# Retention and feed-forward on one core: the opening of the kernel reordered

## Chip, core and metric

The kernel runs on one NeuronCore of a Trainium2 chip. The metric is the device time of one execution in microseconds. The kernel before was timed in three runs; the profile is of a further execution. Engines are named as in the profile: PE is TensorE (PEld its weight loads), DVE VectorE, ACT ScalarE, POOL GpSimd, SP SyncE, which here only issues DMAs.

## What is computed

Attention without softmax and with a decay (retention), then a feed-forward layer of two products with `h - tanh(h)` between them. Batch 8, 8 heads, 576 positions, head size 64, so 4608 tokens of 512 numbers; the hidden size is 2048. All data is float32.

```python
scores = scale * np.matmul(q, k.transpose(0, 1, 3, 2))       # scale = 1/8
gamma = 1.0 - 2.0 ** (-5.0 - np.arange(H))
Dmat = np.where(rel >= 0, gamma[:, None, None] ** rel, 0.0)  # rel = query position - key position
x = np.matmul(scores * Dmat, v)      # then laid out as [tokens, heads * 64]
h = x @ w_in
out = (h - np.tanh(h)) @ w_out
```

## The kernel before

**Blocks and items.** The 576 positions are nine chunks of 64. A block is one chunk for all eight batches, 512 tokens. An item is one chunk of one batch with its eight heads. Items of chunk 0 need no state; later ones use a running state (the sum of k times v over earlier chunks), which is held in SBUF as `state`. Two items of one chunk make a pair; pairs 4 to 7 belong to block 1, pairs 8 to 11 to block 2, and so on. An *entry* (`entry`, line 253) does one pair on TensorE: the scores of the next pair, the outputs of this pair, its share of the state and, where asked for, first states of chunk 0 (`first_states`). Behind it DVE and ACT make the masked scores `pm` and the split output `xh`, `xl`.

**Two words for a number.** TensorE's matmuls here read fp32r. Each operand of the feed-forward products is split into a high word and a low remainder, and three products of these are summed. A hidden step `mm1(n, f)` (line 285) multiplies hidden tile f of 16 for block n: 12 matmuls, then a copy of the result by ACT (line 296) and, for block 0 and most of block 1, a DMA of it to DRAM (the *spill*, line 297), from where it is fetched later. The second product is `mm2` (line 330).

**Weights.** A weight tile is 512 KB, loaded by `load_w` (line 68). ACT makes a mask from it (`guard`, lines 74 and 75); DVE builds the high word in three instructions (lines 83, 88 and 90), ACT copies it (line 93) and DVE makes the low word (line 100). This is one *unit*, given out in three steps by `step()`; the low word of a unit is issued behind line 83 of the next one (`finish`). At its second step a unit also issues the next tile's guard, if that tile's load has been issued by then (line 86); otherwise the next guard comes with the next unit's first step. `stream` lists the 32 tiles, first those of `w_in`.

**Order.** Instructions keep, on every engine, the order in which they are written (`in_order`), and so do the DMAs in an issuing queue. The opening handles chunk 0 item by item (lines 405 to 417), with tile 0 converted between items 4 to 7, then tile 1. Then a list `seq` of 32 hidden steps runs (line 441): block 0's alone for the first `lead` = 10 steps, then block 0's and block 1's in turn. In step k, ahead of `mm1`: loads up to tile k + 5 (from k = 4), scalings of v and k by ACT (`scale_v`, `scale_k`), the first step of unit k + 2; behind it: the other two steps, loads by the table `loads` in steps 0 to 3, and an entry in steps 5, 6, 8 and 9 (the table `early`). The scores of pair 4 and the first states of the first two batches come in step 3. Scaling q of pairs 4 to 8 is POOL's work.

**Tiles that share a place.** Early data lies where the second weights will be later: items of chunk 0 in wo15 down to wo8, decay in wo7, the table for q in wo6, the k rows of chunk 0 in wo4 and wo5, pairs 6 and 7 in wo0 to wo3.

## Time and profile before

| | |
|---|---|
| timed runs | 904.4, 905.46, 903.27 us; median 904.4 us |
| profiled execution | 902.73 us, its span 901.0 us |
| granted TensorE clock, mean | 0.995 |
| PE busy | 880.7 us, 98% of the span |
| DVE / ACT / POOL busy | 367.7 / 288.8 / 74.3 us |
| DMA | 82.06 MB, mean 91 GB/s |

The span runs from the first to the last instruction; 1.7 us of the execution lie around it. Rows of the timeline give the start, the duration, the engine and line, the operation with its output and inputs, and in brackets how long the engine sat idle before it and what ended that. A clock of 1.00 is full speed.

### The profile page before, as it was taken

The page shows a single profiled execution, that of the slowest core. Times are in us where ns is not written, and L with a number is a line of the kernel's source. Part 1 is how long each engine was busy: PE and PEld are TensorE (multiplying, and loading weights), DVE is VectorE, ACT ScalarE, POOL GpSimd, SP SyncE. Part 2 cuts the span into 40 slices and gives each one's busy share as a digit, 9 for nine tenths or more (in the row PEclk, how much of TensorE's full clock was granted, in tenths as well). Part 3 has the DMA queues.
Part 4 walks back from the last instruction along what each step waited for, and adds up shares of the span by engine and source line. Part 5 has one row for each costly group of instructions (what it writes and reads, how often), then busy time and mean ns, then how long its engine had stood idle before and what let it go on. Part 6 is the DMA issues. An engine that isn't in the chain of part 4 may idle for free.

```text
span 901.0 us, 17598 instructions
## 1 busy us (share of the span) xinstructions
PE 880.7 (98%) x7834; PEld 725.5 (81%) x7834; DVE 367.7 (41%) x547; ACT 288.8 (32%) x514; POOL 74.3 (8%) x66
## 2 busy tenths in 40 slices
PE   7879999999999999999999999999999999999997
PEld 5668888878888888888888888888888888888886
DVE  5778968665332333223323332333333322223222
ACT  3668865444222222122222222222222222222222
POOL 0220001120010011111111111110001111000000
PEclk9989999999999999999999999999999999999999
DMA  8975864462311121111311131113110211002001
GB/s 318 330 259 197 292 216 130 153 206 83 95 48 53 40 55 48 53 48 51 91 54 48 47 95 54 48 47 95 48 48 21 77 49 48 1 1 48 1 1 47
DMA packets 30844, 82.06 MB, mean 91 GB/s; under 512 B 3760, under 2 KB 4912, under 8 KB 30768
## 3 DMA queue, kind: packets, MB, share of 16 engines
q1 hardware_dynamic: 30448, 80.41, 27.7%
q8 instruction: 61, 1.00, 0.5%
q10 hardware_dynamic: 320, 0.52, 0.2%
q14 instruction: 15, 0.12, 0.0%
HBM read 63.62 MB, written 17.30 MB: 90 GB/s over the span
## 4 chain that ended last, share of the span: by engine, by line
PE 95%; DMA 1%; DVE 1%; issue 1%; ACT 1%; SPq 0%; DVEq 0%
PE o L343 44%; PE h L291 43%; PE s L218 3%; PE own L218 2%; PE new L218 2%; DMA rwi<-in_w_in_dram 1%; DMA a<-in_first_dram 0%; PE new_first L218 0%; DVE mi L88 0%; PE s_first L218 0%; ACT wi L93 0%; DVE mi L90 0%; DVE ob L358 0%; PE wps L372 0%; ACT mi L74 0%
## 5 line engine op out<-in xcount | busy, mean ns | idle before, releaser
L291 PE MATMUL h<-xh,wi 128*128 128x512 f32 x1152 | 306.3, 391 | 3.7 <-ACT wi L93 2.8
L343 PE MATMUL o<-wo,gh 128*128 128x512 f32 x1152 | 293.4, 393 | 0.4 <-DVE ob L358 0.4
L291 PEld LDWEIGHTS h<-xh,wi 128*128 128x128 f32 x1152 | 216.0, 188 | 50.3 <-ACT wi L93 4.2
L343 PEld LDWEIGHTS o<-wo,gh 128*128 128x128 f32 x1152 | 213.8, 188 | 46.8 <-DVE ob L358 1.5
L305 DVE TENSOR_TENSOR g<-h,g 128x512 f32<-128x512 f32 x114 | 78.8, 691 | 370.2 <-ACT g L304 370.2
L304 ACT ACTIVATE g<-h 128x512 f32<-128x512 f32 x114 | 68.2, 598 | 423.8 <-PE h L291 422.9
L343 PE MATMUL o<-wo,gl 128*128 128x512 f32 x576 | 158.3, 389 | 0.0
L291 PE MATMUL h<-xl,wi 128*128 128x512 f32 x576 | 154.7, 391 | 0.0
L291 PEld LDWEIGHTS h<-xl,wi 128*128 128x128 f32 x576 | 108.7, 189 | 22.8
L343 PEld LDWEIGHTS o<-wo,gl 128*128 128x128 f32 x576 | 108.1, 188 | 22.5
L307 DVE TENSOR_TENSOR gl<-g,gh 128x512 fp32r<-128x512 f32 x114 | 82.4, 723 | 78.2 <-ACT gh L306 71.4
L306 ACT CAST gh<-g 128x512 fp32r<-128x512 f32 x114 | 70.7, 620 | 87.9 <-DVE g L305 87.9
L154 POOL TENSOR_TENSOR a<-a,qtab 128x512 f32<-128x512 f32 x28 | 36.9, 1317 | 637.7 <-DMA a<-in_qkv_dram 571.7
L218 PE MATMUL own<-a,state 64*64 64x64 f32 x960 | 59.2, 221 | 0.0
L218 PE MATMUL own<-pm,a 64*64 64x64 f32 x960 | 57.7, 218 | 0.0
L218 PEld LDWEIGHTS own<-a,state 64*64 64x64 f32 x960 | 47.8, 134 | 0.4 <-issue 0.4
L218 PEld LDWEIGHTS own<-pm,a 64*64 64x64 f32 x960 | 48.0, 135 | 0.0
L218 PEld LDWEIGHTS s<-a 64*64 64x64 f32 x960 | 30.5, 134 | 10.9 <-issue 10.9
L218 PE MATMUL s<-a 64*64 64x64 f32 x960 | 34.7, 221 | 0.3 <-issue 0.3
L327 DVE TENSOR_TENSOR gl<-s,gh 128x512 fp32r<-128x512 f32 x30 | 21.9, 730 | 29.8 <-PE o L343 27.3
L155 POOL TENSOR_TENSOR a<-a,vtab 128x512 f32<-128x512 f32 x28 | 31.4, 1122 | 0.0
L326 ACT CAST gh<-s 128x512 fp32r<-128x512 f32 x30 | 18.7, 622 | 38.6 <-PE o L343 27.9
(57 smaller groups left out, 476.9 us busy)
## 6 DMA issues: line engine op xcount, KB each, us to landing
a<-in_qkv_dram SPq DMA_DIRECT2D x30, 1024.0 KB, 5.3
out_dram<-ob SPq DMA_DIRECT2D x68, 128.0 KB, 2.4
rwi<-in_w_in_dram SPq DMA_DIRECT2D x16, 512.0 KB, 8.2
rwo<-in_w_out_dram SPq DMA_DIRECT2D x16, 512.0 KB, 4.7
spill_dram<-g SPq DMA_DIRECT2D x30, 256.0 KB, 3.1
s<-spill_dram SPq DMA_DIRECT2D x30, 256.0 KB, 2.8
a<-in_first_dram SPq DMA_DIRECT2D x8, 384.0 KB, 6.0
a_early<-in_qkv_dram SPq DMA_DIRECT2D x4, 512.0 KB, 7.2
```

The source lines that it names most:

```text
L154: nc.gpsimd.tensor_tensor(a[:, :, 0], a[:, :, 0], qtabs[c].unsqueeze(1).broadcast_to([P, 2, 4, C]), op=ALU.mult)
L155: nc.gpsimd.tensor_tensor(a[:, :, 2], a[:, :, 2], vtab[:, c].unsqueeze(1).unsqueeze(3).broadcast_to([P, 2, 4, D]), op=ALU.mult)
L218: nc.tensor.matmul(out_, w, x, start=start, stop=stop)
L291: nc.tensor.matmul(hp, win[f][:, a, cc, :], x[:, cc, :], start=(k == 0), stop=(k == 3 * NCC - 1))
L304: nc.scalar.activation(g, h, AF.Tanh)
L305: nc.vector.tensor_tensor(g, h, g, op=ALU.subtract)
L306: nc.scalar.copy(gh, g)
L307: nc.vector.tensor_tensor(gl, g, gh.bitcast(F32), op=ALU.subtract)
L326: nc.scalar.copy(gh, g)
L327: nc.vector.tensor_tensor(gl, g, gh.bitcast(F32), op=ALU.subtract)
L343: nc.tensor.matmul(o[t], g[:, t * P : (t + 1) * P], wout[f][:, a, :], start=(f == first and k == 0), stop=(f == final and k == 2),)
```

## The change

**Opening.** Item 1 and the decay table are loaded from ACT's queue; the activation that loads ACT's table comes after these issues and after the warm-up matmuls. Tile 0 is loaded behind item 3 instead of behind item 4; its guard comes at item 2, its three steps at items 3, 4 and 5. The k rows of the first four batches are loaded ahead of tile 2, and tile 3 is the last load of the opening.

**Order.** `lead` is 13, so block 1's hidden steps begin at step 13 of the list. Entries come in steps 4, 7, 10 and 12; the scores of pair 4 and first states in step 2. Tile 4 is issued in step 0, tile 5 in step 1 and none in step 2; in steps 3 to 8 one tile is issued in each, tile k + 3, behind the spill of the step; from step 9 on, ahead of `mm1`, loads go up to tile k + 4. Pair 5 is loaded in step 0, pair 6 in step 3, pair 7 in step 6, pair 8 in step 8 and pair 9 in step 13. The second k rows come in step 2.

**Engines.** q of pairs 4 to 8 is scaled by DVE, one instruction a pair, in steps 1, 3, 6, 9 and 11. Pairs 6 and 7 are loaded as two tiles that hold both items, one with q and k, one with v and the k rows, so that one instruction spans both items. The k rows are scaled four batches at a time, in steps 1 and 5. The copies of first states into `state` are ACT's.

```diff
+class Parts:
+    def __init__(self, parts):
+        self.parts = parts
+    def __getitem__(self, at):
+        return self.parts[at[1] // 2][at[0], at[1] % 2, at[2], at[3]]
...
-    def prep(p):
+    def prep(p, q=True):
...
+        if q:
+            table = qtabs[c].unsqueeze(1).broadcast_to([P, 2, 4, C])
+            nc.gpsimd.tensor_tensor(a[:, :, 0], a[:, :, 0], table, op=ALU.mult)
...
+        src = qkv_d[c - 1, 2 * pr : 2 * pr + 2].rearrange("u p t i s -> p u t i s")
+        parts = []
+        for t in range(2):
+            parts.append(const.tile([P, 2, 2, 4, C], F32, tag=f"wo{2 * (pr - 2) + t}", name=f"a_early{p}_{t}"))
+            nc.sync.dma_start(parts[t], src[:, :, 2 * t : 2 * t + 2])
         for u in range(2):
-            j = 2 * p + u
-            loaded[j] = const.tile([P, 4, 4, C], F32, tag=f"wo{2 * (pr - 2) + u}", name=f"a_early{j}")
-            nc.sync.dma_start(loaded[j], qkv_d[c - 1, 2 * pr + u])
+            loaded[2 * p + u] = Parts([part[:, u] for part in parts])
+        loaded["qv", p] = parts[0][:, :, 0], parts[1][:, :, 0]
 
     def scale_q(p):
-        if ("pair", p) in loaded:
-            q = loaded["pair", p][:, :, 0]
-            nc.gpsimd.tensor_tensor(q, q, qtabs[1].unsqueeze(1).broadcast_to([P, 2, 4, C]), op=ALU.mult)
-        else:
-            for u in range(2):
-                q = loaded[2 * p + u][:, 0]
-                nc.gpsimd.tensor_tensor(q, q, qtabs[1], op=ALU.mult)
+        q, table = loaded["qv", p][0], qtabs[p // (B // 2)]
+        nc.vector.tensor_tensor(q, q, table.unsqueeze(1).broadcast_to([P, 2, 4, C]), op=ALU.mult)
 
     def scale_v(p):
+        v = loaded["qv", p][1]
         for i in range(4):
-            vs = ...
-            for v in vs:
-                nc.scalar.activation(v, v, AF.Copy, scale=vtab[:, 1, i : i + 1])
+            nc.scalar.activation(v[:, :, i], v[:, :, i], AF.Copy, scale=vtab[:, 1, i : i + 1])
...
-        return ms, lambda: nc.vector.tensor_copy(state[:, b : b + 2], new)
+        return ms, lambda: nc.scalar.copy(state[:, b : b + 2], new)
...
-        elif p < B - 2:
-            load_pair(p + 4)
...
     load_first(0)
-    nc.sync.dma_start(decay, decay_d)
-    for j in range(1, 5):
-        load_first(j)
+    load_first(1, nc.scalar)
+    load_first(2)
+    nc.scalar.dma_start(decay, decay_d)
+    load_first(3)
+    nc.scalar.activation(warm[:, :1], warm[:, :1], AF.Tanh)
     upto("load", 1)
-    for j in range(5, B):
+    for j in range(4, B):
         load_first(j)
     upto("load", 2)
     nc.sync.dma_start(vtab, vtab_d)
+    nc.sync.dma_start(krows[0], krows_d[0])
+    upto("load", 3)
+    load_early(B // 2)
+    nc.sync.dma_start(mask, mask_d)
     upto("load", 4)
-    nc.sync.dma_start(krows[0], krows_d[0])
-    nc.sync.dma_start(mask, mask_d)
-    load_early(B // 2)
...
-        if j == 4:
+        if j == 2:
             upto("guard", 1)
...
-        if 4 <= j < 7:
+        if 3 <= j < 6:
             step()
...
-    lead = 10
+    lead = 13
...
-    early = {5: 4, 6: 5, 8: 6, 9: 7}
-    loads = {0: (6, 5), 1: (7, 6), 2: (8, None), 3: (9, 7)}
-    scale_q(B // 2)
+    early = {4: 4, 7: 5, 10: 6, 12: 7}
+    loads = {0: (5, 5), 1: (6,), 3: (7, 6), 4: (8,), 5: (9,), 6: (10, 7), 7: (11,), 8: (12, 8)}
+    scales = {1: 4, 3: 5, 6: 6, 9: 7, 11: 8}
...
-        if k > 3:
-            upto("load", k + 6)
-        if k == 3:
-            scale_k(0)
+        if k > 8:
+            upto("load", k + 5)
+        if k in (1, 5):
+            scale_k(k // 4)
...
-        if k == 1:
+        if k in scales:
+            scale_q(scales[k])
+        if k in loads:
+            upto("load", loads[k][0])
+            for p in loads[k][1:]:
+                load_early(p) if p < B else load_pair(p)
+        if k == 2:
             nc.sync.dma_start(krows[1], krows_d[1])
-        if k in loads:
-            upto("load", loads[k][0] - 1)
-            if loads[k][1]:
-                load_early(loads[k][1])
-                scale_q(loads[k][1])
-        if k == 3:
             sc = scores_of(B // 2 - 1)
...
-            if p == 5:
-                prep(B)
+        if k == 13:
+            load_pair(B + 1)
         if k == 16:
+            prep(B, False)
             prep(B + 1)
```

## The prediction

> **What bounds the kernel now.** I read the stretches of the span first, then TensorE's timeline for the gaps, then the rows of the engines that end them. The stretches (us; busy time and count of PE, PEld, DVE, ACT, POOL; granted clock, DMA share, GB/s):

> ```profile
> 0.00:18.89 18.89, 14.04 (x282) 9.90 (x283) 8.11 (x20) 6.15 (x14) 0.20 (x4) 1.00 0.91 339
> 18.89:66.09 47.20, 37.78 (x493) 29.75 (x493) 36.05 (x49) 28.60 (x61) 12.20 (x10) 0.93 0.79 288
> 66.09:80.00 13.91, 13.59 (x323) 11.55 (x323) 10.29 (x17) 11.97 (x32) 0.00 (x0) 1.00 0.48 165
> ...
> 50.00:60.00 10.00, 5.42 (x166) 4.58 (x165) 6.20 (x11) 4.57 (x12) 2.26 (x2) 0.77 0.92 332
> 60.00:70.00 10.00, 9.98 (x185) 8.17 (x184) 7.80 (x10) 6.49 (x19) 2.90 (x2) 0.89 0.27 97
> ```

> TensorE is full from about 70 us on, so the change is worth what it does before that. TensorE's timeline (start, duration, what it wrote, idle before it and what ended it):

> ```profile
> 6.04 0.37 PE L218 MATMUL s_first<-a 64*64 64x64 f32 x2 [0.82 <-DMA a<-in_first_dram]
> 15.07 0.33 PE L218 MATMUL s_first<-a 64*64 64x64 f32 x4
> 18.89 1.20 PE L291 MATMUL h<-xh,wi 128*128 128x512 f32 x4 [0.97 <-ACT xh L244]
> 22.95 1.20 PE L291 MATMUL h<-xh,wi 128*128 128x512 f32 x4 [1.04 <-ACT wi L93]
> 32.49 1.15 PE L218 MATMUL s<-a 64*64 64x64 f32 x32
> 35.71 1.68 PE L218 MATMUL new_first<-a,krows 64*64 64x64 f32 x32 [2.08 <-ACT krows L424]
> 44.25 0.27 PE L218 MATMUL s<-a 64*64 64x64 f32 x2
> 47.47 1.20 PE L291 MATMUL h<-xh,wi 128*128 128x512 f32 x4
> 57.45 1.44 PE L218 MATMUL new_first<-a,krows 64*64 64x64 f32 x22 [4.21 <-issue]
> 69.65 1.20 PE L291 MATMUL h<-xh,wi 128*128 128x512 f32 x4
> 75.01 1.19 PE L291 MATMUL h<-xh,wi 128*128 128x512 f32 x4
> 79.68 1.98 PE L291 MATMUL h<-xh,wi 128*128 128x512 f32 x8
> 82.40 1.98 PE L291 MATMUL h<-xh,wi 128*128 128x512 f32 x8
> ```

> From these: one hidden step of a block (mm1, 12 matmuls) costs 82.40 − 79.68 = 2.72 us; an entry 47.47 − 44.25 = 3.2 us, the last one 75.01 − 69.65 − 2.72 = 2.6; scores and first states 1.15 + 1.68 = 2.83. At 75.01 the kernel before has ten mm1 (f = 0 to 9) and all four entries behind it; three dense mm1 more bring it to 83.2 us with mm1 0 to 12 done. I call that the **mark**: the changed kernel has the same work done when its fourth entry ends, and what follows is dense in both. Of 75.01 − 18.89 = 56.1 us, 27.2 + 2.83 + 12.2 = 42.2 are work, so 13.9 are lost. The largest piece is the 4.21 us gap in an entry, which nothing in the profile releases, with the slow clock behind it: 0.77 and 0.89 over 10 us each are 4.6 and 2.2 us at half speed, to about 62.2, and from 57.45 on TensorE loses half of 4.75 to it, 2.4 us.

> **Part 1, the first items.** Two queues can take away the 0.82 us wait at 6.04; item 2 follows at TensorE's own pace. I take 0.4, from 0 (transfers as full as before: the first stretch moves 339 GB/s) to 0.8. Converting weight tile 0 one item sooner takes its instructions out of the last item's way:

> ```profile
> 15.95 0.68 DVE L88 SCALAR_TENSOR_TENSOR mi<-rwi,mi 128x512 int32<-128x512 int32 x1
> 16.55 0.42 DVE L226 TENSOR_TENSOR pm<-s_first,decay 128x256 f32<-128x256 f32 x1
> 17.95 0.62 ACT L93 CAST wi<-mi 128x512 fp32r<-128x512 f32 x1 [1.09 <-DVE mi L90]
> 18.47 0.37 ACT L244 CAST xh<-own_first 128x256 fp32r<-128x256 f32 x1
> ```

> The mask product waited 0.6 for L88, and xh stood behind the weight copy, which DVE released at 17.9. Item 7 runs from 15.07 to 18.89, 3.8 us; without these two it is the scores 0.7, product 0.44, own 0.68, xh 0.42, or 2.3. Gain 1.5 (0.5 if the later place of tile 0's load ahead of items 4 to 7 holds them up). The first mm1 then starts at 18.89 − 0.4 − 1.5 = 17.0, bounds 16.5 to 18.4.

> **Part 2, up to the third mm1.** mm1 1 follows the conversion chain as before, 22.95 − 18.89 = 4.06 behind mm1 0: 21.0. For mm1 2, w3 is now the last transfer of the opening batch, in the place of the 1 MB pair that landed at 23.2:

> ```profile
> 23.21 1.57 POOL L173 TENSOR_TENSOR a<-a,qtab 128x512 f32<-128x512 f32 x1 [22.77 <-DMA a<-in_qkv_dram]
> 23.54 1.78 DVE L88 SCALAR_TENSOR_TENSOR mi<-rwi,mi 128x512 int32<-128x512 int32 x1
> 33.53 0.66 ACT L74 ACTIVATE mi<-rwi 128x512 int32<-128x512 f32 x1 [3.13 <-DMA rwi<-in_w_in_dram]
> 47.09 0.68 ACT L74 ACTIVATE mi<-rwi 128x512 int32<-128x512 f32 x1
> 48.34 0.61 ACT L93 CAST wi<-mi 128x512 fp32r<-128x512 f32 x1
> ```

> A guard takes 48.34 − 47.09 = 1.25 on ACT, and whatever is behind it on ACT waits when its weights are late, as at 33.53. So: w3 at 22.8, guard 3, high copy of tile 2 and with it mm1 2 at 24.7; scores and first states follow without the 2.08 us wait (krows are loaded and scaled earlier), mm1 3 from 30.2 to 32.9. Scaling q on DVE isn't in this trace; by the nearest row, L88 at its undisturbed 0.68 on the same 128x512, it is five times 0.68, or 3.4 us, and it takes away the POOL products beside which L88 took 1.78 (1.1 lost at this one place). Both lie under DVE's waits for guards; without that cover they are about even. The four state copies moved to ACT cost some 0.58 each (the copy of a hidden result, below, has their shape), under ACT's waits for weights; 2.3 us bare. Pairs 6 and 7 come in two transfers each as before, cut by halves of the data instead of by item, so bytes and issues are equal, and scaling v takes four instructions for eight. The later mask, krows1, pair loads (steps 8 and 13) and products on POOL are read long after, or after a DVE row in the same step; cost 0, and up to 1 us if POOL's v products meet full DVE at 80 us.

> **Part 3, loads step by step: the dear part.** In steps 3 to 8 w(k+3) is issued once, after spill k, and no further tile is under way. Since the load is not issued yet when the unit asks for the next guard (line 86), guard k+3 comes first in step k+1, ahead of step k+1's copy of the hidden result on ACT; that copy releases spill k+1, and on SP the next weight load stands behind that spill. So one load, one guard, one copy and one issue form a ring:

> ```profile
> 22.80 0.58 ACT L296 COPY g<-h 128x512 f32<-128x512 f32 x1
> 23.41 0.34 SPq L297 DMA_DIRECT2D spill_dram<-g  x1
> 23.79 0.43 SPq L68 DMA_DIRECT2D rwi<-in_w_in_dram  x1
> 27.63 0.68 ACT L74 ACTIVATE mi<-rwi 128x512 int32<-128x512 f32 x1 [0.44 <-DMA rwi<-in_w_in_dram]
> ...
> rwi<-in_w_in_dram SPq DMA_DIRECT2D x1, 512.0 KB, 3.9
> ...
> a<-in_qkv_dram SPq DMA_DIRECT2D x1, 1024.0 KB, 6.0
> ```

> Landing 3.84 (3.9 at 64.4 us, with nothing else under way), guard 1.25, copy to spill 0.61, spill to load 0.38: **6.1 us a step**. TensorE wants (3 x 2.72 + 3.2) / 3 = 3.8 on average. Before, w8 and w9 were issued ahead of step 4 and the ring did not exist. Counted from mm1 3's end at 32.9 + 0.3: w6 issued 34.2; five rounds, one of them 0.85 longer, since ahead of guard 7 ACT has a copy of entry 4, a state copy and four scalings of krows1 (each 0.37, the width of the xh row): 31.3, so w11 is issued at 65.5 and lands at 69.3. mm1 10 needs tile 10's low half, which is made behind guard 11 and L83:

> ```profile
> 40.75 0.69 DVE L83 SCALAR_TENSOR_TENSOR mi<-rwi,mi 128x512 int32<-128x512 int32 x1 [1.64 <-ACT mi L75]
> 41.36 0.69 DVE L100 TENSOR_TENSOR wi<-mi,wi 128x512 fp32r<-128x512 f32 x1
> ```

> That is 1.25 + 1.3 after the landing, then its last four matmuls, 1.0: mm1 10 ends at 72.9. Next late is w12: it stands behind pair 8 on SP (6.0 to land, 1.3 more for w12), at 73.7; guard 12 is ahead of tile 11's high copy and of v's scaling for entry 6 on ACT, so entry 6 starts at 73.7 + 1.25 + 0.6 + 0.3 = 75.9. Then 3.2 + 2 x 2.72 + 2.6 = 11.2: the mark is reached at 87.1, **3.9 us later** than before. For that the entries stand apart, so the 4.21 us gap goes, and its half clock; but gaps of 2 to 3.5 us come instead. 2.08 us (at 35.71) did not lower the clock, 4.21 did; I put 1.0 us in the sum, from 0 to 4.8, twice the 2.4 that one drop cost.

> [...]

> **Sum.** Profiled execution 902.73 + 3.9 + 1.0 = 907.6. The timed runs are 904.4, 905.46 and 903.27, their median 1.7 above that execution; the mean of all four is 904.0, and from there 4.9 gives **908.9**.

> **Rivals.** *The loads are in time* (the other side): tiles land before anything asks for them, TensorE loses only the 1.3 and 1.0 before mm1 1 and 2, and the mark is at 17.0 + 35.4 + 2.83 + 12.2 + 2.3 = 69.7, 13.5 less: 890.5. For it: nothing is hidden behind a deep queue any more, DMA share falls. Against it: it needs the ring under 3.8 us, and its landing alone takes 3.84. It decides from a ring of 6.1 − 3.9/5 = 5.3 us downward. *Half a ring*: ring 5.3, no change, 904; for it only that one of five tiles could land quicker. *The clock falls often*: each gap halves it and the entries run at half speed, 3.8 more than I have taken: 912.7; for it is 0.77 after one gap, against it the 2.08. *The gap stays*: PE's 2 x 7834 instructions in 61 packets are 257 each,

> ```profile
> q8 instruction: 61, 1.00, 0.5%
> ```

> and two entries close together use up packets fastest, while the DMA share was 0.92; I read the 4.21 as a packet come late. If it is something else, 4.21 + 2.4 of half clock come back: 915.5. [...]

> **How the numbers follow.** Forecast 0.60 (slower), clock falls often 0.12 (slower), gap stays 0.04 (slower), half a ring 0.09 (no change), loads in time 0.15 (faster). A measurement of this kernel tells about 0.2%, 1.8 us. The forecast's own range is 904 to 913.5 (first stage ±1, five rounds of ±0.3, last wait ±1.5, clock −1 to +3.8); 0.02 of its chance fall within 0.2% and 0.02 below. So faster 0.15 + 0.02 = 0.17, same 0.09 + 0.02 = 0.11, slower 0.72. The range is 898.5 to 914: it holds the half ring and an upper bit of the fast case, and leaves out the rest of that (0.13), the gap that stays (0.03) and the tails (0.04).

> **What would show it.** First mm1 near 17; no gap put to issue; guard rows (L74) in 38 to 72 us each with 2 to 3 us idle before them, ended by the weight DMA, some 6 us apart; spill and weight load in pairs on SP; TensorE idle before mm1 6, 7, 9, 10 and entry 6, dense from 76. It is wrong if guards 6 to 11 come under 5 us apart, or if the mark falls before 83.

## The result, and the profile after

The changed kernel takes 917.17 us (median of four runs, 916.4 to 918.51) against 903.84 us (901.92 to 905.46) for the kernel before in the same comparison: a ratio of 1.015, 95% interval 1.0125 to 1.0175, so 13.3 us slower. The forecast had 4.9 us slower, 908.9 us, with 914.0 as its upper end. The profiled execution took 916.44 us, its span 914.7, 13.7 longer than the span before.

Stretches of the changed kernel's span (us; busy time and count of PE, PEld, DVE, ACT, POOL; granted clock, DMA share, GB/s). The bounds are the first hidden step, the issue of weight tile 6, that of tile 11, and the mark:

```profile
0.00:19.55 19.55, 13.32 (x282) 9.73 (x283) 8.19 (x20) 6.13 (x14) 0.20 (x4) 1.00 0.91 350
19.55:36.50 16.95, 15.11 (x118) 11.81 (x119) 13.89 (x22) 12.42 (x23) 0.00 (x0) 1.00 0.61 221
36.50:71.82 35.32, 24.84 (x382) 19.43 (x381) 18.67 (x30) 18.32 (x37) 0.00 (x0) 0.90 0.53 173
71.82:96.79 24.97, 18.79 (x332) 15.41 (x330) 13.37 (x21) 13.05 (x28) 1.04 (x1) 0.79 0.63 216
96.79:130.00 33.21, 33.21 (x150) 27.51 (x147) 30.77 (x46) 25.98 (x46) 3.06 (x2) 1.00 0.84 292
```

From 96.79 us on TensorE is full. The mark stands there, 13.6 us behind the 83.2 of before, which is the whole difference; the dense rest is the same. TensorE's timeline says where it lies (each row: begin, us busy, instruction, and in brackets the idle time ahead of it and what ended it; of timelines only the rows that the text uses are shown):

```profile
5.18 1.33 PE L233 MATMUL s_first<-a 64*64 64x64 f32 x20 [2.10 <-DMA a<-in_first_dram]
19.55 1.20 PE L304 MATMUL h<-xh,wi 128*128 128x512 f32 x4 [0.26 <-ACT xh L259]
50.21 1.20 PE L304 MATMUL h<-xh,wi 128*128 128x512 f32 x4 [3.15 <-DVE wi L110]
58.30 0.27 PE L233 MATMUL s<-a_early 64*64 64x64 f32 x2 [0.78 <-PE h L304]
65.15 1.78 PE L233 MATMUL new_first<-a,krows 64*64 64x64 f32 x32 [4.40 <-issue]
83.83 0.37 PE L233 MATMUL own<-pm,a_early 64*64 64x64 f32 x2 [2.67 <-ACT a_early L194]
88.73 1.45 PE L304 MATMUL h<-xh,wi 128*128 128x512 f32 x4
```

The first hidden step is 0.66 us later than before, not 1.9 earlier. A wait of 3.15 us for the low word of a weight tile (line 110) stands within a hidden step, and a gap of 4.40 us put to issue stands within entry 5, as one of 4.21 did before. Entry 6 goes on at 83.83 us, when v is scaled, and ends at 88.73. Now the guards of tiles 6 and 12 on ACT (line 84), the copy of a hidden result behind the first of them (line 309), and the issues of weight tiles 6 to 11 on SP (line 78):

```profile
40.26 0.67 ACT L84 ACTIVATE mi<-rwi 128x512 int32<-128x512 f32 x1 [1.14 <-DMA rwi<-in_w_in_dram]
...
41.50 0.57 ACT L309 COPY g<-h 128x512 f32<-128x512 f32 x1
...
81.64 0.66 ACT L84 ACTIVATE mi<-rwi 128x512 int32<-128x512 f32 x1 [4.05 <-DMA rwi<-in_w_in_dram]
...
36.50 0.43 SPq L78 DMA_DIRECT2D rwi<-in_w_in_dram  x1
42.48 0.43 SPq L78 DMA_DIRECT2D rwi<-in_w_in_dram  x1
49.70 0.43 SPq L78 DMA_DIRECT2D rwi<-in_w_in_dram  x1
55.81 0.43 SPq L78 DMA_DIRECT2D rwi<-in_w_in_dram  x1
61.80 0.43 SPq L78 DMA_DIRECT2D rwi<-in_w_in_dram  x1
71.82 0.43 SPq L78 DMA_DIRECT2D rwi<-in_w_in_dram  x1
```

The ring is there: tiles 6 to 10 follow each other by 5.98, 7.22, 6.11 and 5.99 us (6.1 and, with the scaling of krows1, 6.95 were forecast), and the last round takes 10.0, since the gap put to issue falls into it. One round in full: tile 6 is issued at 36.50, its guard starts at 40.26, the copy at 41.50, and tile 7 is issued at 42.48. The guards of tiles 6, 8 and 11 wait 1.14, 1.47 and 3.71 us for their weights. Those of tiles 7, 9 and 10 come right behind other work of ACT, so the load's landing isn't alone in filling the 6 us. And the granted clock, in the same columns as above:

```profile
50.00:60.00 10.00, 7.58 (x109) 5.55 (x112) 4.64 (x8) 4.61 (x10) 0.00 (x0) 0.83 0.59 189
60.00:70.00 10.00, 5.60 (x91) 4.74 (x83) 5.67 (x9) 4.24 (x8) 0.00 (x0) 0.83 0.45 155
80.00:90.00 10.00, 6.98 (x165) 6.39 (x165) 5.61 (x10) 6.34 (x13) 1.04 (x1) 0.53 0.57 215
```

The lowest clock in any 1 us of these stretches is 0.50. At this half speed 0.83, 0.83 and 0.53 are 3.4, 3.4 and 9.4 us, where before had 6.8 in one piece (0.50 in each 1 us from 56 to 62).

### The profile page after: what moved, and what is told of

Same layout as the page of the kernel before. It is cut to its first block, busy times and chain, and to the rows that moved or that the text cites. A ratio compares the mean times of both kernels' runs of the same rounds, so it can differ in the third digit from the quotient of the medians.

```text
span 914.7 us, 17581 instructions
## 1 busy us (share of the span) xinstructions
PE 884.2 (97%) x7833; PEld 728.1 (80%) x7834; DVE 363.2 (40%) x548; ACT 288.1 (32%) x502; POOL 67.0 (7%) x59
## 3 DMA queue, kind: packets, MB, share of 16 engines
q10 hardware_dynamic: 608, 1.05, 0.3%
## 4 chain that ended last, share of the span: by engine, by line
PE 92%; DMA 3%; ACT 1%; DVE 1%; issue 1%; SPq 0%; ACTq 0%; DVEq 0%
PE o L356 43%; PE h L304 40%; DMA rwi<-in_w_in_dram 3%; PE s L233 3%; PE own L233 2%; PE new L233 2%; DMA decay<-in_decay_dram 1%; ACT mi L84 0%; PE own_first L233 0%; PE new_first L233 0%; ACT g L309 0%; DVE mi L93 0%; DVE ob L371 0%; DVE mi L100 0%; PE s_first L233 0%
## 5 line engine op out<-in xcount | busy, mean ns | idle before, releaser
L320 DVE TENSOR_TENSOR gl<-g,gh 128x512 fp32r<-128x512 f32 x114 | 80.5, 706 | 78.2 <-ACT gh L319 71.3
## 6 DMA issues: line engine op xcount, KB each, us to landing
a<-in_qkv_dram SPq DMA_DIRECT2D x30, 1024.0 KB, 5.2
rwi<-in_w_in_dram SPq DMA_DIRECT2D x16, 512.0 KB, 4.9
rwo<-in_w_out_dram SPq DMA_DIRECT2D x16, 512.0 KB, 4.7
a_early<-in_qkv_dram SPq DMA_DIRECT2D x4, 512.0 KB, 6.1
```

The lines of the kernel that those rows point to most:

```text
L320: nc.vector.tensor_tensor(gl, g, gh.bitcast(F32), op=ALU.subtract)
```

## The experiments

Every kernel was timed against the kernel before on the same chip; the ratios carry the comparison.

| kernel | median us | before us | ratio, 95% interval |
|---|---|---|---|
| the change | 917.17 | 903.84 | 1.015 (1.0125 to 1.0175) |
| deeper loads | 902.59 | 904.44 | 0.9984 (0.9969 to 0.9998) |
| guard behind | 915.18 | 904.44 | 1.0132 (1.011 to 1.0153) |
| one queue | 917.34 | 904.44 | 1.0154 (1.0131 to 1.0177) |
| stream moved by 40 | 913.49 | 904.44 | 1.0109 (1.0088 to 1.0129) |
| pair 7 later | 914.17 | 903.47 | 1.012 (1.0096 to 1.0143) |
| deeper loads, moved by 60 | 900.9 | 903.47 | 0.9974 (0.996 to 0.9988) |
| the same, one queue | 901.52 | 903.47 | 0.9982 (0.9969 to 0.9995) |
| before, moved by 60 | 906.12 | 903.47 | 1.0017 (1.0003 to 1.0031) |
| deeper loads, moved by 32 | 898.0 | 903.04 | 0.9945 (0.9928 to 0.9963) |
| the same, decay alone on ACT's queue | 897.75 | 903.04 | 0.9933 (0.9918 to 0.9947) |
| before with the change's loads | 910.61 | 903.04 | 1.008 (1.0065 to 1.0096) |

**Deeper loads.**

```diff
-    loads = {0: (5, 5), 1: (6,), 3: (7, 6), 4: (8,), 5: (9,), 6: (10, 7), 7: (11,), 8: (12, 8)}
+    loads = {0: (5, 5), 1: (6,), 2: (7,), 3: (8, 6), 6: (0, 7), 8: (0, 8)}
...
-        if k > 8:
-            upto("load", k + 5)
+        if k > 3:
+            upto("load", k + 6)
```

> The changed kernel with its weight loads issued as far ahead as before (tile k + 4 in steps 0 to 3, up to tile k + 5 ahead of each later step), all else as changed. Ring theory (one load, one guard, one copy and one issue a step, 6.1 us): the guards of tiles 6 to 11 no longer wait 1 to 4 us each for their weights, TensorE runs at its own pace. Work left after the fourth hidden step's start (31.4 + 2.7 = 34.1 us): 9 x 2.72 + 12.2 = 36.7, with the 4.4 us gap put to issue and its half clock (2.4) still there and some 1 us of small waits 78.6, where the changed kernel had 96.8: some 18 us less, 897 to 902 timed. Rival (the transfers themselves are the limit, whatever their order, or the entries' new places cost the time): 910 to 917.

902.59 us, 14.6 under the change: the weight loads' order alone costs that. That is a little above the 897 to 902 expected. Against the kernel before it is 0.16% faster, at the edge of what can be told. So all the other parts of the change together brought nothing that shows. ACT's guards of tiles 7 to 9 in this run, and what is left on TensorE:

```profile
41.40 0.68 ACT L84 ACTIVATE mi<-rwi 128x512 int32<-128x512 f32 x1 [1.25 <-DMA rwi<-in_w_in_dram]
46.91 0.67 ACT L84 ACTIVATE mi<-rwi 128x512 int32<-128x512 f32 x1 [0.62 <-DMA rwi<-in_w_in_dram]
49.14 0.67 ACT L84 ACTIVATE mi<-rwi 128x512 int32<-128x512 f32 x1
...
59.18 1.97 PE L233 MATMUL new_first<-a,krows 64*64 64x64 f32 x32 [5.13 <-DMA rwi<-in_w_in_dram]
```

These guards stand 5.5 and 2.2 us apart and wait little. The gap in entry 5 is still there, 5.13 us; the profile puts it to a weight transfer that ended in it, though these matmuls read no weights.

**Guard behind the hidden step.**

```diff
-        if last_two < 0:
-            step()
-        else:
+        if last_two >= 0:
             fetch(*late[2 + last_two])
         mm1(n, f, ("h", "o2", "h", "o3")[k % 4] if k < len(seq) - 4 else "h")
+        if last_two < 0:
+            step()
```

> The changed kernel with the unit's first step behind the hidden step instead of ahead of it, so that ACT copies the hidden result before the next guard; loads as changed. Ring theory: the guard (1.25) leaves the ring of loads; a tile's load then follows the end of a hidden step by 1.0 us and the low word needed by the hidden step after next comes 6.5 us later, about 4.2 us a step instead of 6.1. Five rounds save 9 us, of which the issue gap may take some back: 906 to 911 timed, weight issues on SP 4 to 5 us apart. Rival (the guard's place on ACT does not matter, one load a step is slow by itself): 915 to 918, weight issues still 6 apart.

915.18 us: 2.0 less, where I had expected 6 to 11. Tiles 6 and 11 are issued 33.2 us apart instead of 35.3. ACT's timeline shows why:

```profile
48.83 0.67 ACT L84 ACTIVATE mi<-rwi 128x512 int32<-128x512 f32 x1
...
52.85 0.62 ACT L103 CAST wi<-mi 128x512 fp32r<-128x512 f32 x1 [2.69 <-DVE mi L100]
53.65 0.58 ACT L309 COPY g<-h 128x512 f32<-128x512 f32 x1 [0.18 <-PE h L304]
54.13 0.68 ACT L84 ACTIVATE mi<-rwi 128x512 int32<-128x512 f32 x1
```

The copy of the hidden result (53.65) no longer stands behind the guard of its step, but behind the previous unit's high copy (52.85), which waits for DVE, which waits for that unit's guard (48.83). A ring stays, 5.3 us here from guard to guard, but it goes through another engine, and neither of these guards waits for its weights. That loads issued so late keep the guards apart in both forms, since no unit can ask for the next guard early, is argued and not shown here.

Nor are the 2.0 us clearly the ring's. In the profiled runs, 1.4 us apart, the gap in entry 5 is 2.48 us instead of 4.40: ahead of it this run is 0.5 us behind the change (61.28 against 60.75), behind it 1.4 us ahead (63.76 against 65.15).

**The opening on one queue.**

```diff
     load_first(0)
-    load_first(1, nc.scalar)
-    load_first(2)
-    nc.scalar.dma_start(decay, decay_d)
+    nc.sync.dma_start(decay, decay_d)
+    load_first(1)
+    load_first(2)
     load_first(3)
```

> The changed kernel with all opening loads on SP in the order of before (item 0, decay, items 1 to 3), tile 0 and what follows as changed. Theory: the two queues shared the transfer rate, item 0 landed at 5.1 instead of 4.0 us and the decay table at 6.9 instead of 4.3, so that the first masked product began at 6.95 instead of 5.27. With one queue the first product is back at 5.3, the first hidden step starts 1 to 1.7 us earlier than 19.55 and the kernel takes 1 to 2 us less: 915 to 916. Rival (the later items' landing behind tile 0 sets the first hidden step): first hidden step within 0.5 us of 19.55, 917.

The first masked product (DVE) of the change and of this run, and then this run's first hidden step, its wait for the high word of weight tile 4, and two stretches:

```profile
6.95 0.42 DVE L241 TENSOR_TENSOR pm<-s_first,decay 128x256 f32<-128x256 f32 x1 [5.82 <-DMA decay<-in_decay_dram]
```

```profile
5.17 0.42 DVE L241 TENSOR_TENSOR pm<-s_first,decay 128x256 f32<-128x256 f32 x1 [4.04 <-PE s_first L233]
...
17.99 1.20 PE L304 MATMUL h<-xh,wi 128*128 128x512 f32 x4 [0.26 <-ACT xh L259]
...
34.63 1.33 PE L304 MATMUL h<-xh,wi 128*128 128x512 f32 x4 [1.87 <-ACT wi L103]
...
30.00:40.00 10.00, 8.13 (x80) 5.97 (x83) 4.47 (x7) 4.63 (x11) 0.00 (x0) 0.83 0.64 214
50.00:70.00 20.00, 14.65 (x185) 11.08 (x186) 10.29 (x17) 8.87 (x17) 0.00 (x0) 0.68 0.50 167
```

On one queue the product comes 1.8 us and the first hidden step 1.56 us earlier, 0.9 ahead of the kernel before. The time stays at 917.34 all the same. When tile 6 is issued, only 0.55 of the 1.56 us are left (35.95 us against 36.50). The guard of tile 5, which on ACT stands ahead of the high copy of tile 4, has waited 3.74 us for its load, 2.61 in the change. So TensorE waits 1.87 us at 34.63 where the change waits 0.79 at 35.19. At the issue of tile 11 nothing is left (71.94 against 71.82). TensorE's clock in 50 to 70 us is 0.68 in this run, 0.83 in the change; that this took the rest is likely and not shown.

**TensorE's stream moved by 40 instructions.**

```diff
     busy(WARM, P)
+    busy(20, C)
```

> The changed kernel with 20 more warm-up matmuls of 64 columns, that is 40 more instructions ahead in TensorE's stream, in a time in which it waits for item 0. Theory of alignment: the 4.4 us gap put to issue comes when a packet of 256 instructions is asked for just as an entry begins (record 1216 of TensorE in both kernels) and the entry has used up the one before (at record 1472) ahead of the packet. Moved by 40, the packet is asked for 40 records ahead of the entry, some 4 us sooner: gap below 1 us, guard round of tile 11 back to 6.1, no half clock at 65 us, 4 to 7 us less: 910 to 913. Rival (something stops TensorE at record 1472 whatever stands there): a gap of over 4 us at record 1472, now 40 records earlier within the entry, 917.

913.49 us, 3.7 less; expected were 4 to 7, 910 to 913. Entry 5 runs through in 61.99 − 58.78 = 3.2 us, with no gap:

```profile
58.78 0.27 PE L233 MATMUL s<-a_early 64*64 64x64 f32 x2 [0.77 <-PE h L304]
61.02 1.04 PE L233 MATMUL new_first<-a,krows 64*64 64x64 f32 x30
61.99 1.20 PE L304 MATMUL h<-xh,wi 128*128 128x512 f32 x4
```

So no instruction of the entry is slow by itself. How many TensorE records stand ahead of the gap can be read from stretches that begin at 0 and end within it, here the kernel before and then the change (columns as above):

```profile
0.00:55.00 55.00, 43.18 (x728) 32.81 (x729) 37.09 (x59) 32.13 (x68) 7.24 (x10) 1.00 0.88 322
```

```profile
0.00:62.00 62.00, 46.59 (x729) 35.35 (x730) 34.73 (x61) 33.05 (x66) 0.20 (x4) 0.97 0.71 255
```

1457 and 1459 matmuls and weight loads (728 and 729, 729 and 730): the same place in the stream to within two, though not at the same matmul of the entry (22 of the 32 `new_first` are still to come in the kernel before, all 32 in the change). (With the 16 and 13 other records of TensorE ahead of the gap, semaphore instructions and a drain, that is 1473 and 1472, the 1472 of the expectations. Entry 5 of the change begins with record 1217, so 256 stand between its begin and the gap.) The next packet of instructions, in the change, by its DMA queues (transfers, MB, share): the data between 58.3 (the begin of the entry) and 62.7 us, and then the instructions from 62.7 to 63.9:

```profile
q1 hardware_dynamic: 669, 1.35, 89.3%
```

```profile
q8 instruction: 1, 0.02, 5.2%
```

It came through only behind 1.35 MB of data, and moved for 1.0 us (5.2% of 16 engines' 1.2 us), from 62.8 to 63.8; 1.4 us after that TensorE goes on (65.15).

**Pair 7 one step later.**

```diff
-    loads = {0: (5, 5), 1: (6,), 3: (7, 6), 4: (8,), 5: (9,), 6: (10, 7), 7: (11,), 8: (12, 8)}
+    loads = {0: (5, 5), 1: (6,), 3: (7, 6), 4: (8,), 5: (9,), 6: (10,), 7: (11, 7), 8: (12, 8)}
```

> The changed kernel with pair 7 (1 MB) issued in step 7 instead of step 6, so that its transfer starts behind the request for TensorE's packet at record 1216 and not ahead of it; nothing else. Theory: the packet's delay in the gap (asked for at 58.3, begun at 62.8 us) is the queue of data that it stands in; with it gone the packet begins 1 to 2 us after the request, gap 4.4 shrinks to 0 to 1.5, no half clock there: 3 to 6 us less, 911 to 914. Rival (the packet's delay has nothing to do with the data under way, only its place decides): gap still over 4 us, 916 to 918.

914.17 us, 3.0 less, at the upper end of what was expected, and the gap is 1.52 instead of 4.40:

```profile
63.01 1.15 PE L233 MATMUL new_first<-a,krows 64*64 64x64 f32 x32 [1.52 <-issue]
```

So 2.88 of the 4.40 us went with the place of pair 7's data, which I read as the packet's wait for it; that what is left comes of the entry using up a packet faster than the next one comes at all is not shown by itself.

**Deeper loads with the stream moved by 60, on two queues and on one, and the kernel before moved by 60.**

```diff
-    busy(WARM, P)
+    busy(WARM + 30, C)
```

> The deeper loads of the first run, and 60 more instructions at the start of TensorE's stream (46 warm-up matmuls of 64 columns instead of 16 of 128). Theory: ring and packet gap are independent; from 902.6 the gap of 5.1 us, its half clock (2.4) and perhaps the 1.05 us gap at 83.7 go: 894 to 897, faster than both kernels. Rival (the gap is only moved, another packet runs short elsewhere): 900 to 903.

> The same with the opening loads on one queue in the order of before. Opening theory (first hidden step 1.5 us earlier on one queue, which in the run on one queue alone was eaten by half clock behind the waits for weights): with no such waits the 1.5 us stay: 893 to 895.5. Rival (the next transfers are no earlier and take it back): as the run beside it, 894 to 897.

> The kernel before with the same 60 more instructions at the start of TensorE's stream. Record 1216 then falls some 38 records ahead of its entry 5, 4 to 5 us ahead of need instead of 2. Alignment theory: its 4.2 us gap shrinks below 2.5 us, and the half clock with it or in part: 899 to 902 against 904. Rival (something stops TensorE at record 1472 whatever stands there): gap 4 us, 904.

All three missed what was hoped: 900.9 and 901.52 us, and 906.12 for before. The gap was moved, not removed. The run with two queues, then before moved by 60:

```profile
46.81 0.39 PE L304 MATMUL h<-xl,wi 128*128 128x512 f32 x1 [3.34 <-issue]
72.81 0.48 PE L233 MATMUL new_first<-a,krows 64*64 64x64 f32 x3 [3.05 <-issue]
...
0.00:46.50 46.50, 35.39 (x601) 27.66 (x603) 29.35 (x53) 26.46 (x53) 0.20 (x4) 1.00 0.86 307
0.00:72.50 72.50, 58.34 (x984) 46.74 (x986) 48.94 (x84) 43.94 (x88) 1.25 (x5) 0.97 0.85 298
```

```profile
55.06 0.69 PE L218 MATMUL new_first<-a,krows 64*64 64x64 f32 x6 [3.52 <-issue]
...
0.00:54.50 54.50, 40.22 (x601) 31.52 (x602) 32.53 (x52) 28.11 (x60) 7.40 (x10) 0.87 0.82 301
```

They now stop at 1204 and 1203 matmuls and weight loads, 255 and 254 sooner than the 1459 of the change and the 1457 of before: one packet, by the 257 instructions that the 61 packets hold on average. There the packet begins, by this count, within entry 4 and is used up at that entry's end (before) or in the hidden step behind it (two queues). The second gap, at 72.81 us, stands at 1970, 766 or three packets further on. All these places fit one grid of 256 records to within two, and by it the next two runs were laid out. Nothing in these two runs tells more of the opening: one queue and two are the same within their intervals.

**Moved by 32, and the decay table alone on ACT's queue.**

```diff
-    busy(WARM, P)
+    busy(2 * WARM, C)
...
     load_first(0)
-    load_first(1, nc.scalar)
-    load_first(2)
     nc.scalar.dma_start(decay, decay_d)
+    load_first(1)
+    load_first(2)
     load_first(3)
```

> Deeper loads, and TensorE's stream moved by 32 instructions (32 warm-up matmuls of 64 columns in the place of 16 of 128, the same time). Packets of 256 then begin at records 960, 1216 and so on, and by the traces so far a packet is asked for when the one before it begins and takes up to 5 us beside 1 MB loads. Counted with 2.4 us for 256 records of an entry and 0.113 us a record in hidden steps, every packet now has 5 us or more (moved by 60, the ends at 1216 and 1984 had 2 to 3 and gaps of 3.0 and 3.3 came). Theory: no gap put to issue over 1 us, the clock stays full from about 11 us, 4.4 + 3 us less than the run moved by 60: 894 to 897. Rival (a packet runs short somewhere at any place): gaps of 3 us again, 900 to 902.

> The same, and of the opening only the decay table on ACT's queue, items 0 to 3 on SP. Opening theory: item 0 no longer shares its transfer with item 1, so lands near 4.1 us and decay near 4.3; first product near 5.3 instead of 6.95, first hidden step 1 to 1.5 us earlier: 893 to 896, 1 us under the run beside it. Rival (what follows is set by later transfers or by the clock): no difference, 894 to 897.

898.0 and 897.75 us: 0.55% and 0.67% under the kernel before, faster than both kernels. The largest gap put to issue that is left is 1.8 us in the first. It stands ahead of the last six state products (`new`) of an entry, at 2224 matmuls and weight loads, 1020 or four packets behind 1204. The clock is full from 40 to 90 us (1.00 in each 10 us). TensorE's longest wait for issue in the first run (us, count, longest), and its clock in 70 to 80 us; then the second run's first masked product, which came 1.0 us earlier than in the first (6.91 there):

```profile
PE new L233 <- issue: 1.8, 1, 1.8
...
70.00:80.00 10.00, 8.23 (x154) 6.73 (x153) 7.10 (x13) 6.45 (x14) 0.00 (x0) 1.00 0.50 164
```

```profile
5.90 0.42 DVE L241 TENSOR_TENSOR pm<-s_first,decay 128x256 f32<-128x256 f32 x1 [4.76 <-PE s_first L233]
```

Both were a little above what was expected, 894 to 897 and 893 to 896. Between the two kernels the 0.25 us say nothing: 1 us of the opening is less than these runs tell apart.

**The kernel before with the change's weight loads alone.**

```diff
-    loads = {0: (6, 5), 1: (7, 6), 2: (8, None), 3: (9, 7)}
+    loads = {0: (6, 5), 1: (7, 6), 3: (8, 7), 4: (9, None), 5: (10, None), 6: (11, None), 7: (12, None), 8: (13, None)}
...
-        if k > 3:
-            upto("load", k + 6)
+        if k > 8:
+            upto("load", k + 5)
```

> The kernel before with the weight loads of the change alone: tile 4 in step 0, tile 5 in step 1, one tile (k + 3) in each of steps 3 to 8 behind the spill, up to tile k + 4 from step 9 on. Entries, opening and engines as before. Ring theory: rounds of 6.1 us and more (pairs 8 and 9 go between them) from step 3 on; tile 11 is issued some 32 to 36 us behind tile 6 instead of within 16, and ends behind what the entries and the gap cost anyway: 906 to 912 against 904. Rival (the ring only costs together with the entries' new places): 903 to 905.

910.61 us, 0.8% slower, 7.6 us. Four of its weight issues, with pairs 8 and 9 between them on the same queue:

```profile
46.62 0.43 SPq L68 DMA_DIRECT2D rwi<-in_w_in_dram  x1
54.06 0.43 SPq L68 DMA_DIRECT2D rwi<-in_w_in_dram  x1
61.42 1.08 SPq L68 DMA_DIRECT2D rwi<-in_w_in_dram  x1
68.41 1.01 SPq L68 DMA_DIRECT2D rwi<-in_w_in_dram  x1
```

7.0 to 7.4 us apart: the late loads make a kernel slower by themselves. In the change they cost 14.6.

## Why the prediction was wrong

**Direction and mechanism held.** The ring of load, guard, copy and issue was forecast at 6.1 us a step and measured at 6.0 to 6.1 (7.2 with krows1), and issuing the loads earlier gives back 14.6 us. The place of the last wait held as well: entry 6 starts 12.0 us after tile 11's issue (83.83 for 71.82; 10.4 forecast), behind guard 12, which waits 4.05 us for tile 12.

**The size was wrong.** The mark was forecast at 87.1 and came at 96.8, 9.7 us later, by these steps:

- *Part 1, "the first mm1 then starts at 17.0": 2.55 us, of which 2.3 are left when tile 6 is issued (36.5 for 34.2).* The step took two queues as a gain of 0 to 0.8. They cost 1.56: items 0 and 1 are both issued at 0.74 us, item 0 is used at 5.18 instead of 4.10, and the product waits for the decay table until 6.95. The lower bound should have been a loss: the first stretch moved 339 GB/s before and moves 350 in the change, so I read the later item 0 as what item 1 took. The rest of the opening, with tile 0 converted earlier, brought 0.9 (first hidden step at 17.99 on one queue against 18.89), where 1.5 was put in for the conversion alone.
- *Part 3, "five rounds ... 31.3": 4.0 us.* The rounds were right but the one in which the gap of 4.40 stood, 10.0 us.
- *Part 3, "the entries stand apart, so the 4.21 us gap goes": this step failed.* I had read the gap rightly as a packet of instructions come late, but had taken its cause to be two entries in a row. It is where a packet's boundary lies, as the moved streams show (3.2 us and no gap in entry 5, moved by 40): in the change the entry began where, by the count, a packet begins and used it up in about 2.4 us (58.30 to 60.75, where the gap starts), and the next one moved only from 62.8, behind 1.35 MB of data. The profile shows when a packet moves and not when it is asked for; that this is at the boundary before is my reading. In the kernel before the gap stood at 1457 records, in the change at 1459; lines were moved so that the entry's begin fell on the boundary (record 1217; 1195 before). The rival *the gap stays* had this outcome, with 0.04. Its time, 915.5, is the nearest of all that I gave, but that is luck: it had the reason wrong, and 5.7 of the 9.7 us come from the other steps.
- *The last wait, "6.0 to land, 1.3 more for w12": 1.6 us.* Guard 12 starts 9.8 us after tile 11's issue (81.64 for 71.82), where 8.2 was put in. Tile 13 is issued in one go with tile 12, which the sum left out; that this is the reason is not shown.
- *The last stretch, 13.0 for 11.2 us: 1.8.* Its first 6 us lie in 80 to 90 us, at a clock of 0.53, and entry 6 takes 4.9 us (83.83 to 88.73) instead of 3.2. I had put 1.0 us of clock into the sum, an estimate from two gaps of the kernel before (2.08 us, clock full; 4.21 us, half), for gaps of 2 to 3.5 us that might not lower it. In the change the clock is 0.50 in 52 to 55 us and again in 80 to 89 us, behind gaps of 3.15 us that end at 50.21 and 78.49.

2.3 + 4.0 + 1.6 + 1.8 = 9.7, and without the 1.0 of clock that the sum held 8.7; the profiled execution took 8.8 more than the 907.6 of the sum.

**Other points.** Scaling q on DVE, state copies on ACT and halves by data cost nothing that shows, as forecast: with deeper loads they are all in the kernel of 902.59. They show no gain either; none of them was tested alone.

## What to carry to other kernels

Before loads are thinned out to "just in time", follow what a load's issue waits for: if it stands behind a store that waits for a copy that stands behind work on the previous load, one load's whole round trip can become the period, as it did here, with 6.0 to 7.2 us at a DMA share of 0.53. In a stream with bursts of short instructions on TensorE, count where the instruction packets begin (here 61 for 2 x 7834 instructions, 257 each), and try large transfers at another place than just ahead of a burst (the 1 MB pair one step later took the gap from 4.40 to 1.52 us); 32 dummy instructions more ahead of them were worth some 3.5 us here (0.9984 to 0.9945 in ratio to the kernel before, on two chips). The second issuing queue cost the first transfer here: item 0 was used at 5.18 us instead of 4.10, and the time was the same on one queue (917.34 us for 917.17).
